# Moving the stores of converted weights from SyncE's DMA queue to GpSimd's

## The chip, the cores and the metric

One core of a Trainium2 chip runs the whole program. The metric is the device time of one execution in microseconds; lower is better. The engines named below are PE (TensorE), DVE (VectorE), ACT (ScalarE), POOL (GpSimd) and SP (SyncE, which here only issues DMAs).

## The reference

Attention over 4 batches and 8 heads of 576 positions with 64 columns, under a banded mask (32 positions wide in half of the heads; every fourth of 128 positions in the others), then two layers of matrix products on the 2304 tokens:

```
scores = scale * np.matmul(q, k.transpose(0, 1, 3, 2))      # masked, softmax
x = attn @ v                                                # -> (2304, 512)
x = (x @ w_a) * (x @ w_b) @ w_out                           # d_ff 1536
h = x @ w_in                                                # d_ff 2048
out = (max(h, 0) + alpha * min(h, 0)) @ w_out2
```

The weights of the two layers arrive as 64-bit floats. The kernel turns them into 32-bit floats on the chip, and each 32-bit number into a high and a low part, so that a product is three matmuls (high by high, high by low, low by high).

## The kernel before

The tokens are cut into tiles of 512, 512, 512 and 768. Attention of the first 512 tokens comes first; then the first layer runs over tile 0, 1 and 2 (12 blocks `f` of 128 columns of d_ff each), and the attention of the next tile is done in between, in 12 groups per tile. After that come the first layer for the last 768 tokens and the second layer for all of them, both by another scheme of products on halves.

While tile 0 is computed, the first layer's weights are converted, block by block: 24 pieces of `w_a` and `w_b` (two for each `f`, `job_w`) and 12 of `w_out` (`job_o`), 36 conversions in all. One conversion (`convert`) is: a load of 512 KB into one of four places of `raw_ring` (L194, issued by SP, kept in program order among the loads); two ACT passes over it (L176, L179) and two DVE passes (L183, L186) that leave 32-bit floats in one of five places of `cf_ring`; the split into high (ACT, L244) and low (DVE, L247) parts, in buffers from which PE reads; and then `then`, a store to DRAM. For `job_w` the 32-bit floats go to `wad` (L258, 256 KB, read from the place in `cf_ring`), for `job_o` the split pair goes to `wod` (L268, 512 KB, read from one of two places of `wo_ring`). Both are read back later: `wod` for tiles 1 to 3 (L277, L629), `wad` for the last tile (L597).

A place of `cf_ring` is written again by the L176 of the fifth conversion after it, a place of `wo_ring` by the L244 of the next but one `job_o`; both must wait until the store has read it.

SP's queue also carries the attention's inputs, in three places each: `in_qk` (L288) and `in_v` (L293). A load for the group three ahead can go only when PE has read that place, so SP stands at these for PE. An attention group is: scores (PE, L324), masking and maximum (DVE, L334, L340), exponentials (ACT, L345), normalisation (DVE, L352 to L354), transposition (PE, L361, into a tile named `tp`), copy (ACT, L366), product with v (PE, L374), placement (DVE, L399). From the second tile on, `visit` puts the transposition of one group, the values of the group before it and the scores of the next side by side on PE; this text calls that a visit, and names it by its `tp`.

The program is written as numbered steps, and a scheduler turns it into one fixed instruction order for each engine, from its own estimate of when inputs are ready. Each engine then runs its order strictly, waiting at semaphores. The tile names in the orders below: `pa`, `pb` and `accA` are PSUM banks, `sa` the bank that values and scores of a visit share, `ft` and `rt` the two large SBUF buffers.

Of the kernel before, what the change touches and what calls it, by code (L numbers as in the profile page):

```python
# [10 lines left out]
F32 = mybir.dt.float32  # L11
# [49 lines left out]
def tile_kernel(ctx: ExitStack, tc: tile.TileContext, qk, v, mask, wab, wo1, w2, alpha, out):  # L61
    nc = tc.nc
# [5 lines left out]
    wod = dram.tile([NFA, 128, 1024], F32, name="wod")  # L68
    wad = dram.tile([NFA, 128, 1024], F32, name="wad")
# [18 lines left out]
    def cut(t, first, *dims):  # L88
        size = int(np.prod(dims))
        ap = t[:, first:first + size]  # L90
        if len(dims) == 2:
            ap = ap.rearrange("p (a b) -> p a b", b=dims[1])
        elif len(dims) == 3:
            ap = ap.rearrange("p (a b c) -> p a b c", b=dims[1], c=dims[2])
        return ap
# [101 lines left out]
    def convert(src, dest, then=None, raws=raw_ring, places=cf_ring):  # L197
        raw = load_raw(src, raws)
        yield
        yield  # L200
        for f in float_of(raw, places):
            yield
        hi, lo = dest()
        split(hi, lo, f, nc.scalar, nc.vector)
        if then:
            then(f)
# [42 lines left out]
    ws, wo = {}, {}  # L249

    def job_w(k, f, j):
        def dest():
            if j == 0:
                ws[f] = cut(rt, 4096 + 2048 * f, 4, 512)
            return ws[f][:, 2 * j], ws[f][:, 2 * j + 1]

        def then(x):
            nc.sync.dma_start(out=wad[f, :, j * 512:(j + 1) * 512], in_=x)  # L258

        queue.append((k, convert(wab[f, j], dest, then)))  # L260

    def job_o(k, f):
        def dest():
            wo[0, f] = w = wo_ring.next().rearrange("p (h n) -> p h n", h=2)
            return w[:, 0], w[:, 1]

        def then(_):
            nc.sync.dma_start(out=wod[f], in_=wo[0, f].rearrange("p h n -> p (h n)").bitcast(F32))  # L268

        queue.append((k, convert(wo1[f], dest, then)))  # L270

# [636 lines left out]
```

## Time and profile before

| | us |
|---|---|
| median of 3 runs (lowest, highest) | 922.96 (922.65, 928.92) |
| the profiled execution, its time | 922.74 |
| the profiled execution, its span on the core | 920.8 |

The span is counted from the first to the last instruction of the core; the 1.94 us between span and time lie outside of it. Busy times of the profile are per engine; engines run side by side, so they don't add up. "Idle before ... <-" names what ended a wait.

### The profile page before, as it was taken

The numbers are of one execution on the slowest core, as the hardware profiler recorded it, in microseconds if no ns is written. First come the engines' busy times: TensorE is split into PE (matmuls) and PEld (weight loads), VectorE is DVE, ScalarE is ACT, GpSimd is POOL, SyncE is SP. The second block draws the span as 40 slices with busy tenths as digits, with TensorE's granted clock in tenths as the row PEclk, the third lists the DMA queues.
The fourth block names the chain that finished last, engine by engine and source line by source line (L and its number), as shares of the span: only waits on it lengthen the run. The fifth ranks groups of instructions, "written<-read, shape, count | busy, mean of one in ns | idle before, by whom it ended". The sixth has DMA issues, their size and how long they took to land.

```text
span 920.8 us, 15175 instructions
## 1 busy us (share of the span) xinstructions
PE 903.7 (98%) x5569; PEld 815.4 (89%) x5572; DVE 620.4 (67%) x1317; ACT 417.4 (45%) x967; POOL 0.7 (0%) x6
## 2 busy tenths in 40 slices
PE   8899999999999999999999999999999999999997
PEld 5677887887877888899999998999999999999997
DVE  5989986667666754669877589768565575555432
ACT  5887885555545543445445356233222242222221
POOL 0000000000000000000000000000000000000000
PEclk9999999999999999999999999999999999999999
DMA  7789895686777743553321988457434435344100
GB/s 212 250 286 331 303 335 200 197 278 222 237 257 263 234 163 109 204 199 132 129 93 67 331 287 297 140 158 231 126 115 142 121 115 161 115 145 129 59 35 34
DMA packets 76585, 171.24 MB, mean 186 GB/s; under 512 B 8672, under 2 KB 23776, under 8 KB 76512
## 3 DMA queue, kind: packets, MB, share of 16 engines
q1 hardware_dynamic: 76512, 170.28, 56.0%
q8 instruction: 44, 0.72, 0.3%
q14 instruction: 29, 0.24, 0.1%
HBM read 133.55 MB, written 36.70 MB: 185 GB/s over the span
## 4 chain that ended last, share of the span: by engine, by line
PE 85%; DMA 7%; DVE 4%; ACT 3%; issue 1%; SPq 0%; ACTq 0%; DVEq 0%
PE at L694 11%; PE pb L694 7%; PE pa L694 7%; PE accB L439 7%; PE accB L440 7%; PE accB L438 7%; PE accA L438 5%; PE accA L439 5%; PE accA L440 5%; DMA ft<-in_w 4%; PE pa L438 3%; PE pa L440 3%; PE pb L438 3%; PE pa L439 3%; PE pb L440 3%; PE pb L439 3%
## 5 line engine op out<-in xcount | busy, mean ns | idle before, releaser
L244 ACT CAST rt<-ft 128x512 fp32r<-128x512 f32 (+2 forms) x288 | 158.7, 560 | 271.0 <-PE accB L440 170.6
L247 DVE TENSOR_TENSOR rt<-ft,rt 128x512 fp32r<-128x512 f32 (+2 forms) x288 | 174.6, 613 | 121.1 <-ACT rt L244 109.0
L694 PE MATMUL at<-rt 128*128 128x384 f32 x648 | 130.9, 335 | 0.7 <-ACT ft L708 0.4
L438 PE MATMUL accB<-rt 128*128 128x384 f32 x384 | 127.6, 335 | 2.1 <-ACT ft L749 1.1
L439 PE MATMUL accB<-rt 128*128 128x384 f32 x384 | 128.4, 334 | 0.6 <-DVE rt L247 0.6
L440 PE MATMUL accB<-rt 128*128 128x384 f32 x384 | 128.0, 334 | 0.0
L694 PEld LDWEIGHTS at<-rt 128*128 128x128 f32 x648 | 113.8, 188 | 1.7 <-ACT ft L708 1.0
L708 ACT COPY ft<-at 128x384 f32<-128x384 f32 x108 | 51.6, 479 | 88.2 <-PE at L694 86.2
L438 PE MATMUL accA<-rt 128*128 128x512 f32 (+1 forms) x240 | 89.2, 373 | 0.5 <-ACT ft L749 0.5
L694 PE MATMUL pb<-rt 128*128 128x384 f32 x432 | 87.3, 336 | 1.2 <-DVE ft L705 1.2
L439 PE MATMUL accA<-rt 128*128 128x512 f32 (+1 forms) x240 | 88.4, 368 | 0.0
L440 PE MATMUL accA<-rt 128*128 128x512 f32 (+1 forms) x240 | 88.1, 368 | 0.0
L694 PE MATMUL pa<-rt 128*128 128x384 f32 x432 | 87.1, 334 | 0.0
L694 PEld LDWEIGHTS pb<-rt 128*128 128x128 f32 x432 | 75.5, 188 | 3.2 <-DVE ft L705 3.1
L694 PEld LDWEIGHTS pa<-rt 128*128 128x128 f32 x432 | 76.0, 188 | 0.0
L438 PEld LDWEIGHTS accB<-rt 128*128 128x128 f32 x384 | 71.9, 188 | 3.2 <-ACT ft L749 1.4
L439 PEld LDWEIGHTS accB<-rt 128*128 128x128 f32 x384 | 72.1, 188 | 1.0 <-DVE rt L247 1.0
L440 PEld LDWEIGHTS accB<-rt 128*128 128x128 f32 x384 | 72.0, 188 | 0.0
L183 DVE SCALAR_TENSOR_TENSOR ft<-ft 128x512 uint32<-128x512 uint32 x68 | 46.8, 689 | 28.5 <-ACT ft L179 27.9
L345 ACT ACTIVATE ft<-ft 128x96 f32<-128x96 f32 x144 | 52.4, 365 | 24.3 <-DVE ft L340 24.0
L705 DVE TENSOR_TENSOR ft<-ft,pb 128x384 f32<-128x384 f32 x72 | 39.7, 552 | 31.5 <-ACT ft L708 31.3
L176 ACT ACTIVATE ft<-ft 128x512 f32<-128x512 f32 x68 | 45.4, 668 | 29.0 <-DMA ft<-in_w 23.2
(80 smaller groups left out, 1377.0 us busy)
## 6 DMA issues: line engine op xcount, KB each, us to landing
rt<-wsd SPq DMA_DIRECT2D x168, 256.0 KB, 3.0
rt<-wod SPq DMA_DIRECT2D x48, 512.0 KB, 3.9
ft<-in_w SPq DMA_DIRECT2D x32, 512.0 KB, 5.0
wsd<-rt SPq DMA_DIRECT2D x56, 256.0 KB, 2.9
ft<-in_wab SPq DMA_DIRECT2D x24, 512.0 KB, 5.9
ft<-in_qk SPq DMA_DIRECT2D x48, 208.0 KB, 3.2
ft<-in_v SPq DMA_DIRECT2D x48, 144.0 KB, 3.2
wad<-ft SPq DMA_DIRECT2D x24, 256.0 KB, 5.0
```

The source lines that it names most:

```text
L176: nc.scalar.activation(f, high.bitcast(F32), AF.Abs, scale=2.0 ** -112)
L183: nc.vector.scalar_tensor_tensor(out=fi, in0=fi, scalar=3, in1=low, op0=ALU.logical_shift_left, op1=ALU.bitwise_or)
L244: hi_eng.copy(hi, x)
L247: lo_eng.tensor_tensor(out=lo, in0=x, in1=hi.bitcast(F32), op=ALU.subtract)
L345: nc.scalar.activation(self.et[:, s], self.st[:, s], AF.Exp, bias=self.sm[:, 0, s:s + 1], accum_out=self.sm[:, 1, s:s + 1])
L438: nc.tensor.matmul(acc, lhsT=wh, rhs=rh, start=first, stop=False)
L439: nc.tensor.matmul(acc, lhsT=wh, rhs=rl, start=False, stop=False)
L440: nc.tensor.matmul(acc, lhsT=wl, rhs=rh, start=False, stop=last)
L694: nc.tensor.matmul(acc[:, :HT], lhsT=a, rhs=x[:, b, c], start=start and c == k == 0, stop=c == 1 and k == 2, skip_group_check=not start,)
L705: nc.vector.tensor_tensor(out=out, in0=x, in1=acc[:, :HT], op=ALU.add)
L708: nc.scalar.copy(out, acc[:, :HT])
```

## The change

The two `then` functions issue their stores on POOL's queue (`nc.gpsimd`) instead of SP's (`nc.sync`). Sizes, places, sources and the place in the program text are the same.

```diff
 def job_w(k, f, j):
     ...
         def then(x):
-            nc.sync.dma_start(out=wad[f, :, j * 512:(j + 1) * 512], in_=x)
+            nc.gpsimd.dma_start(out=wad[f, :, j * 512:(j + 1) * 512], in_=x)
     ...
 def job_o(k, f):
     ...
         def then(_):
-            nc.sync.dma_start(out=wod[f], in_=wo[0, f].rearrange("p h n -> p (h n)").bitcast(F32))
+            nc.gpsimd.dma_start(out=wod[f], in_=wo[0, f].rearrange("p h n -> p (h n)").bitcast(F32))
```

The scheduler, which estimates anew, also gives other orders on the compute engines for a stretch of the program: on ACT, DVE and PE the orders are the same up to the last groups of the first attention and again from the end of tile 0 on, and differ in between.

On SP, the place of the third load of a conversion (the first `in_wab` row here) and of the fourth, before:

```order
L288 DMA ft<-in_qk 128x416 x2
L258 DMA wad<-ft 128x512
L293 DMA ft<-in_v 96x384
L194 DMA ft<-in_wab 128x512
L293 DMA ft<-in_v 96x384
L288 DMA ft<-in_qk 128x416
L258 DMA wad<-ft 128x512
L194 DMA ft<-in_wab 128x512
```

And the same place on SP in the changed kernel:

```order
L288 DMA ft<-in_qk 128x416
L194 DMA ft<-in_wab 128x512
L293 DMA ft<-in_v 96x384
L288 DMA ft<-in_qk 128x416
L293 DMA ft<-in_v 96x384
L288 DMA ft<-in_qk 128x416
L194 DMA ft<-in_wab 128x512
```

The stores are gone; the third load has moved ahead of an `in_qk` and an `in_v` load as well, while the fourth still follows the same `in_v` and `in_qk` loads.

On ACT, at the end of the first attention, one piece of the difference (L176 and L179 are the passes of the third conversion, L345 with the L366 of `tp_8` belong to attention groups):

```order
 L179 ACTIVATE ft<-ft 128x512
 L366 COPY ft<-tp_7_356 96x384
+L176 ACTIVATE ft<-ft 128x512
+L179 ACTIVATE ft<-ft 128x512
 L345 ACTIVATE ft<-ft 128x96 x3
 L366 COPY ft<-tp_8_395 96x384
 L244 CAST rt<-ft 128x512
-L176 ACTIVATE ft<-ft 128x512
-L179 ACTIVATE ft<-ft 128x512
```

The third conversion's two passes now stand ahead of three exponentials and the copy of `tp_8`, where before they stood behind them.

On PE, in tile 0, the visit that begins with `tp_3`, before:

```order
L439 MATMUL accA_3_662<-rt 128x512
L440 MATMUL accA_3_662<-rt 128x512
L438 MATMUL pa<-rt 128x512
L361 MATMUL tp_3_832<-ident,ft 96x128 x3
L374 MATMUL sa_836<-ft 64x64 x6
L324 MATMUL sa_836<-ft 64x96 x6
L439 MATMUL pa<-rt 128x512
```

And the same visit on PE in the changed kernel:

```order
L438 MATMUL pb<-rt 128x512
L439 MATMUL pb<-rt 128x512
L361 MATMUL tp_3_832<-ident,ft 96x128 x3
L374 MATMUL sa_836<-ft 64x64 x6
L324 MATMUL sa_836<-ft 64x96 x6
L440 MATMUL pb<-rt 128x512
L438 MATMUL accA_0_659<-rt 128x512
```

The visit has moved from behind the 12 products into `accA` and one into `pa` to ahead of them, 14 matmuls of 512 columns earlier. Counted so, the visits of tile 0 from `tp_0` to `tp_9` stand 4 later, then 4, 7, 14, 10, 5 and 9 earlier, the same, 8 earlier, and the same; the last two, `tp_10` and `tp_11`, haven't moved.

## Rows read from the trace of the kernel before

**Rows 1.** The page, part 1: busy us of each engine.

```profile
span 920.8 us, 15175 instructions
...
PE 903.7 (98%) x5569; PEld 815.4 (89%) x5572; DVE 620.4 (67%) x1317; ACT 417.4 (45%) x967; POOL 0.7 (0%) x6
```

**Rows 2.** Windows: stretch, its length, busy us (count) by engine, clock, DMA share, GB/s.

```profile
20.00:30.00 10.00, 8.57 (x106) 5.91 (x104) 9.51 (x33) 8.48 (x29) 0.00 (x0) 1.00 0.82 258
30.00:80.00 50.00, 47.49 (x333) 36.00 (x333) 44.09 (x108) 40.88 (x106) 0.00 (x0) 1.00 0.86 289
80.00:140.00 60.00, 60.00 (x394) 48.52 (x392) 54.68 (x121) 49.24 (x118) 0.00 (x0) 1.00 0.90 316
140.00:160.00 20.00, 20.00 (x116) 15.88 (x115) 13.66 (x29) 10.22 (x22) 0.00 (x0) 1.00 0.55 198
```

**Rows 3.** Waits of SP's queue, 0 to 160 us: total us, times, longest.

```profile
SPq L268 <- DVE rt L247: 29.5, 12, 4.7
...
SPq L258 <- DVE ft L353: 9.7, 7, 2.4
```

**Rows 4.** Timeline of SP around the third and fourth load: start, us, what.

```profile
23.80 1.32 SPq L288 DMA_DIRECT2D ft<-in_qk  x2
25.17 0.43 SPq L258 DMA_DIRECT2D wad<-ft  x1
25.70 0.37 SPq L293 DMA_DIRECT2D ft<-in_v  x1
26.11 0.46 SPq L194 DMA_DIRECT2D ft<-in_wab  x1
...
29.68 0.36 SPq L258 DMA_DIRECT2D wad<-ft  x1
30.09 0.42 SPq L194 DMA_DIRECT2D ft<-in_wab  x1
```

**Rows 5.** Timeline of ACT at the same place.

```profile
26.39 0.65 ACT L176 ACTIVATE ft<-ft 128x512 f32<-128x512 f32 x1
...
27.49 0.46 ACT L366 COPY ft<-tp 96x384 f32<-96x384 f32 x1
29.08 0.37 ACT L345 ACTIVATE ft<-ft 128x96 f32<-128x96 f32 x1 [1.13 <-DVE ft L340]
...
30.17 0.45 ACT L366 COPY ft<-tp 96x384 f32<-96x384 f32 x1
```

**Rows 6.** DMA issues (issuer, count, KB, median us to landing), then in_wab's minimum, median, maximum.

```profile
ft<-in_wab SPq DMA_DIRECT2D x24, 512.0 KB, 5.9
...
wad<-ft SPq DMA_DIRECT2D x24, 256.0 KB, 5.0
...
DMA to landing us min/median/max: 3.5/5.9/7.9
```

**Rows 7.** Timeline of PE at its waits; idle time before in brackets.

```profile
30.68 0.57 PE L374 MATMUL ap<-ft 96*64 96x64 f32 x12 [1.03 <-ACT ft L366]
...
34.12 0.50 PE L438 MATMUL pa<-rt 128*128 128x512 f32 x1 [0.31 <-ACT rt L453]
...
37.09 0.50 PE L438 MATMUL acc<-rt 128*128 128x512 f32 x1 [0.28 <-ACT rt L244]
...
77.54 0.39 PE L440 MATMUL pb<-rt 128*128 128x512 f32 x1
77.77 0.39 PE L438 MATMUL accA<-rt 128*128 128x512 f32 x1
79.03 0.50 PE L361 MATMUL tp<-ident,ft 128*96 128x128 f32 x3 [0.88 <-DVE ft L354]
```

**Rows 8.** Timeline of DVE: end of a group's chain; last read of a conversion.

```profile
78.43 0.46 DVE L354 TENSOR_TENSOR ft<-ft 128x288 f32<-128x288 f32 x1
...
126.58 0.69 DVE L186 SCALAR_TENSOR_TENSOR ft<-ft 128x512 uint32<-128x512 uint32 x1
```

**Rows 9.** Timeline of ACT: the fifth conversion after that one.

```profile
138.20 0.67 ACT L176 ACTIVATE ft<-ft 128x512 f32<-128x512 f32 x1
```

## The prediction

> **What bounds the kernel now.** I read the page's busy line first: PE is busy 903.7 of a span of 920.8 us, at a share of 98% [rows 1], so whatever a change gives back must be taken from the 17.1 us in which PE is idle, and whatever it costs must show as new idle time on PE. The windows then say where the stretch of the change stands [rows 2]: the first of the 36 stores goes at 25.17 [rows 4], and the conversions still run at 138 [rows 9]. From 80 us on PE has no idle time there at all, at the full granted clock; between 20 and 30 us it idles 1.43 us and between 30 and 80 us 2.51 us. DVE is the next engine: it has 5.91 us free of 50 and then 5.32 of 60. The DMA engines are 0.86 to 0.90 busy. SP's own waits come third: it stood 29.5 us at `wod` stores and at least 9.7 us at `wad` stores, waiting for DVE [rows 3], with loads queued behind it. Last I read PE's waits one by one: none names a DMA; they name ACT and DVE work that stands late in the conversions or in an attention group [rows 7].
>
> **What the change can give.** It removes 36 issues of 0.36 to 0.43 us [rows 4] from SP, and the waits in front of them. SP isn't on the path to the end, so this is worth only what an earlier load is worth. The loads don't run free: they still stand behind `in_qk` and `in_v` loads that wait for PE, and each needs one of four raw places that DVE's L186 must have left. The fourth load shows the size: behind its `in_v` and `in_qk` loads, SP is free at 29.68 instead of 30.09, 0.4 us earlier [rows 4]. The third gains more, because the new order also puts it ahead of an `in_v` and an `in_qk` load: the first of the two `in_qk` rows at 23.80 takes some 0.4 us as its neighbours do, so the load goes at about 24.2 instead of 26.11 [rows 4].
> The end of the gain is the idle time that PE has from its wait at 30.68 on: 2.51 us in 30 to 80 plus the 0.35 of that wait that lie before 30, against none at the other end. Two of these waits are for casts of weights, 0.31 and 0.28 us [rows 7]; I take these two as gone, **-0.6 us**, since half a microsecond of earlier loads is just enough for them, and leave the attention's waits to the terms below. From 80 to 160 us an earlier load buys nothing: PE is full there.
>
> **What the new ACT order costs.** ACT now meets the third conversion's L176 right after the copy at 27.49, that is at 27.95, and behind it stand the exponentials that before began at 29.08 and the copy at 30.17, whose end PE waited for at 30.68 [rows 5, 7]. An `in_wab` load lands 3.5 to 7.9 us after its issue, 5.9 in the median [rows 6]. Issued at 24.2 it is there at 27.7, 30.1 or 32.1. The two passes take 1.10 us (26.39 to 27.49, [rows 5]). So the exponentials begin at 29.08 as before, or at 31.2, or at 33.2: 0, 2.1 or 4.1 us later, and PE, which idles there already, waits that much longer. In return this conversion itself is earlier (its L176 was behind all that). Between 0 and 2.1 I take **+1.5 us**, nearer the median landing, because the queue ahead of this load is shorter than the median one's by a store; 0 and +4.1 stay as ends.
>
> **What the new PE order costs.** PE takes the visits of tile 0 earlier. A visit's transposition needs the group's L354 on DVE, and how close that is shows at 79.03, where PE waited 0.88 us for an L354 that ended at 78.89 [rows 7, 8]. A matmul of 512 columns takes 0.23 us (77.54 to 77.77, [rows 7]). What counts is the stretch between two visits, from one group's scores to its transposition: counted in the two orders, from `tp_0` to `tp_8` it shrinks by 8, 3 and 7 matmuls, grows by 4 and 5, shrinks by 4, grows by 9, shrinks by 8. On DVE the same groups have 10, 8, 6, 3, 5, 8, 4, 7 conversion and product passes between L334 and L354 before and 7, 6, 5, 6, 7, 6, 5, 4 after, so most of the shorter stretches have a shorter chain to fit, at 0.69 us of DVE for a pass [rows 8]. Twice it doesn't fit: `tp_3` loses 7 matmuls (1.6 us) for one pass (0.7), 0.9 us late; `tp_4` gains 4 (0.9) for three more passes (2.1), 1.2 late. Against that stands the 0.88 us wait at 79.03, which is the wait at `tp_4` and is in part the same time: 0.9 + 1.2 - 0.88 leaves 1.2, and I take **+0.9 us**, since DVE's passes overlap their neighbours a little. The ends are -0.9 (that wait goes and nothing comes) and, if the chains weren't shortened at all, the sum of what shrinks, 30 matmuls, +6.9.
>
> **What the stores cost on POOL.** POOL has 0.7 us of work in the whole program [rows 1], so nothing queues there but the stores themselves, in the order in which the conversions end. The trace shows no DMA issued by POOL. From below the nearest row is SP's issue, 0.36 us; from above the whole landing of a store, 5.0 us [rows 4, 6]. What covers either: a place of `cf_ring` is written again by the fifth conversion after it. The closest of these that I found among 31 is an L186 that ends at 127.27 with the next L176 in the place at 138.20 [rows 8, 9], 10.9 us, so a store may take 5.9 us more than the median 5.0 before ACT waits for it; `wo_ring`'s places have more. Waits added on ACT and DVE are for these places only. `wad` and `wod` are read back only after the last conversion. I cost this at **0**, with the ends under the rivals.
>
> **Sum.** 922.74 for the profiled execution, -0.6 +1.5 +0.9 = **924.5 us**; the median of the runs stands 0.2 us above the profiled one, which I neglect. That is no change: a measurement of this kernel can tell about 1% (9.2 us).
>
> **Rivals.**
> *Faster.* The third load lands before ACT needs it, the waits at casts and the 0.88 us go, and no visit is late. For it speaks that the orders were made for each other; against it, that PE has only 2.9 us to give. Time: 922.74 - 2.5 = 920.2, at best 919.9.
> *Visits wait.* DVE's chains keep their old length because DVE is at 88 to 91% and takes its rows late, and PE stalls at each shrunken stretch: +6.9 +1.5 = 931.1. It decides from the point where L354 ends later than the matmuls ahead of it, which at 79.03 it did already. Against it: the shorter DVE chains counted above.
> *Stores late.* If a store issued by POOL takes over 10.9 us from L186 to landing, ACT waits at L176, and PE runs dry behind it. At 15 us that is 4.1 us over for one round of five places, seven rounds, 29 us at most and some 14 if half is hidden: 937. The Trainium skill's page "SBUF — State Buffer" (the box on the DVE trap) speaks for it: descriptors of a POOL-issued DMA are written by the GpSimd cores, which certain DVE copies lock out, and it tells of a transfer of 620 ns taking 3100 ns. By that figure, as an estimate, a store would be 2.5 us later, within the 5.9 above; no trace here shows it.
> *DVE held.* POOL's preparation of a store blocks DVE, which has 11.2 us free between 30 and 140 us [rows 2]. It decides from 11.2 / 36 = 0.31 us a store. At an SP issue of 0.43 us it costs 36 x 0.43 - 11.2 = 4.3 (927); at 1.5, between that and the 5.0 of a landing, 43 (966). Nothing in this trace shows DVE sharing anything with POOL, which is idle. The same page of the Trainium skill (Who interferes with whom) says that a DVE instruction with two SBUF inputs contends with a GpSimd instruction that reads SBUF, not with one that only writes it. The conversions' DVE passes are of that two-input kind; so by that rule the chance is small, and no run here shows it yet.
> *Without effect.* The raw places, not the stores, hold the loads, and the orders come out even: 922.7, inside the forecast's own range.
>
> **How the numbers follow.** Forecast with its ends (922 to 928): 0.56, the case without effect included. Faster (919 to 922): 0.17. Visits wait (928 to 933.7 with the ACT term at its end): 0.15. Stores late 0.06, DVE held 0.06. Over 932.2 lie most of the last two and a little of the visits: 0.12. Under 913.7 nothing of the above reaches: 0.01. The rest, 0.87, is within 1%. The range 919 to 931 leaves out the last two cases and the upper part of the visits, some 0.16.
>
> **What would show it.** In the profile of the changed kernel: a second DMA queue with 12.6 MB; no L258 or L268 among SP's waits; ACT's idle before the third L176 naming `in_wab`, and PE's wait at the copy of `tp_8` near 32 us instead of 30.68; PE waits for L354 at `tp_3` and `tp_4`; PE without idle time from 90 to 160 us; DVE's pass L186 still at 0.69 us. I am wrong if ACT's L176 or L244 wait for stores, if DVE's passes are longer, or if PE's busy time itself changes.

## The result and the profile after

The changed kernel takes 935.52 us (median of 4 runs, 933.55 to 937.24); the kernel before, 923.11 in the same series. The ratio is 1.0112, with a 95% interval of 1.0085 to 1.0138: it is slower by about 1.1%, 11 us over the forecast and 4.5 us over the end of its range. The profiled execution took 933.55.

The page, part 1, as in [rows 1]:

```profile
span 931.8 us, 15181 instructions
...
PE 909.4 (98%) x5572; PEld 817.5 (88%) x5572; DVE 617.7 (66%) x1317; ACT 417.4 (45%) x967; POOL 20.2 (2%) x42
```

The span grew by 11.0 us. PE is idle 22.4 us of it for 17.1, and its busy time is 5.7 us longer with the same matmuls (three of them, some 0.6 us, are missing from the record of before), which no idle time explains. Windows show where both lie, as [rows 2] did (busy us and count of PE, PEld, DVE, ACT, POOL; then granted clock, DMA share, GB/s):

```profile
30.00:160.00 130.00, 119.23 (x777) 92.05 (x776) 104.21 (x246) 94.90 (x234) 18.87 (x35) 0.97 0.79 270
...
34.00:36.00 2.00, 1.44 (x20) 1.33 (x22) 1.82 (x6) 1.85 (x9) 0.00 (x0) 0.54 0.27 111
36.00:38.00 2.00, 2.00 (x13) 1.43 (x12) 1.65 (x9) 0.36 (x2) 0.00 (x0) 0.50 0.38 120
38.00:40.00 2.00, 2.00 (x6) 1.20 (x4) 0.00 (x0) 1.50 (x4) 0.00 (x0) 0.50 0.19 63
40.00:42.00 2.00, 2.00 (x18) 1.60 (x18) 1.91 (x6) 1.72 (x8) 0.00 (x0) 0.75 0.03 9
```

Between 30 and 160 us PE is idle 130 - 119.23 = 10.8 us, where before it was 2.5 [rows 2]: 8.3 us. From 34 to 42 it ran at half to three quarters of its clock: 1.44 x 0.46 + 2 x 0.50 + 2 x 0.50 + 2 x 0.25 = 3.2 us. Together 11.5 us, some of which later stretches gave back. Of the 5.7 us of longer busy time, 3.2 are the clock's here and some 0.6 the missing records; I haven't placed the rest. The DMA engines moved less per microsecond there than before, not more.

ACT's timeline at the third conversion, for [rows 5]:

```profile
27.04 0.67 ACT L176 ACTIVATE ft<-ft 128x512 f32<-128x512 f32 x1
...
28.14 0.48 ACT L366 COPY ft<-tp 96x384 f32<-96x384 f32 x1
31.88 0.66 ACT L176 ACTIVATE ft<-ft 128x512 f32<-128x512 f32 x1 [3.26 <-DMA ft<-in_wab]
...
34.05 0.46 ACT L366 COPY ft<-tp 96x384 f32<-96x384 f32 x1
```

SP's timeline ahead of it, for [rows 4]:

```profile
24.45 0.43 SPq L288 DMA_DIRECT2D ft<-in_qk  x1
24.92 1.51 SPq L194 DMA_DIRECT2D ft<-in_wab  x1
26.54 0.38 SPq L293 DMA_DIRECT2D ft<-in_v  x1
```

And PE's timeline behind it and at the visits, for [rows 7]:

```profile
34.56 0.91 PE L374 MATMUL ap<-ft 96*64 96x64 f32 x12 [4.26 <-ACT ft L366]
...
38.64 0.63 PE L438 MATMUL pb<-rt 128*128 128x512 f32 x1
39.06 0.63 PE L439 MATMUL pb<-rt 128*128 128x512 f32 x1
39.49 0.63 PE L440 MATMUL pb<-rt 128*128 128x512 f32 x1
...
53.61 0.53 PE L361 MATMUL tp<-ident,ft 128*96 128x128 f32 x3 [0.59 <-DVE ft L354]
...
71.66 0.50 PE L361 MATMUL tp<-ident,ft 128*96 128x128 f32 x3 [1.31 <-DVE ft L354]
...
96.95 0.50 PE L361 MATMUL tp<-ident,ft 128*96 128x128 f32 x3 [1.62 <-DVE ft L354]
```

The reader sees one chain: the third load goes at 24.92, nearly as forecast, takes 1.51 us to issue and is there some 6.9 us after its start; ACT stands 3.26 us at L176 with the exponentials and the copy of `tp_8` behind it; PE waits 4.26 us for that copy, 3.2 more than the 1.03 of before. The same twelve matmuls that took 0.57 us at 30.68 [rows 7] then show 0.91.

This wait isn't the only one of its kind. ACT's waits for the loads of conversions, 0 to 180 us (total, times, longest), and SP's waits in the same stretch:

```profile
ACT ft L176 <- DMA ft<-in_wab: 17.2, 13, 3.3
...
ACT ft L176 <- DMA ft<-in_wo: 5.9, 5, 1.8
```

```profile
SPq L293 <- PE sa L374: 60.5, 12, 7.8
SPq L194 <- DVE ft L186: 18.9, 12, 3.6
```

Eighteen conversions make ACT wait 23.1 us in all. Before, in the same stretch, the same two lines came to 2.8 us:

```profile
ACT ft L176 <- DMA ft<-in_wo: 2.5, 2, 2.1
...
ACT ft L176 <- DMA ft<-in_wab: 0.3, 1, 0.3
```

No store stands among SP's waits any more, where [rows 3] had 39 us of them. Between 30 and 160 us no wait listed for PE or DVE names a DMA; the late loads reach them through ACT.

The stores themselves, by the DMA issues (issuer, count, KB, median us to landing), for [rows 6]:

```profile
ft<-in_wab SPq DMA_DIRECT2D x24, 512.0 KB, 5.7
...
wad<-ft POOLq DMA_DIRECT2D x24, 256.0 KB, 5.4
...
wod<-rt POOLq DMA_DIRECT2D x12, 512.0 KB, 5.1
```

And one line of the view on L258, and one of that on L186, where the three times are minimum, median and maximum in ns:

```profile
L258 POOL DMA_DIRECT2D wad<-ft x24: 539/539/684, 25.3 to 146.4; - x24
```

```profile
L186 DVE SCALAR_TENSOR_TENSOR ft<-ft x68: 681/685/694, 24.3 to 589.5; 128x512 uint32<-128x512 uint32 x68
```

A store takes POOL 0.54 us and lands in 5.4 or 5.1 us; DVE's pass is as long as it was [rows 8]. Nobody waited for a store.

### The profile page after: what moved, and what is told of

Its sections match the earlier page's. It is cut to its first block, busy times and chain, and to the rows that moved or that the text cites. A ratio compares the mean times of both kernels' runs of the same rounds, so it can differ in the third digit from the quotient of the medians.

```text
span 931.8 us, 15181 instructions
## 1 busy us (share of the span) xinstructions
PE 909.4 (98%) x5572; PEld 817.5 (88%) x5572; DVE 617.7 (66%) x1317; ACT 417.4 (45%) x967; POOL 20.2 (2%) x42
## 4 chain that ended last, share of the span: by engine, by line
PE 83%; DMA 9%; DVE 4%; ACT 3%; issue 1%; SPq 0%; ACTq 0%; DVEq 0%
PE at L694 11%; PE pb L694 7%; PE pa L694 7%; PE accB L439 7%; PE accB L440 7%; PE accB L438 7%; PE accA L438 5%; PE accA L439 4%; PE accA L440 4%; DMA ft<-in_wab 3%; PE pb L438 3%; PE pa L438 3%; PE pb L439 3%; PE pb L440 3%; PE pa L440 3%; DMA ft<-in_w 3%
## 5 line engine op out<-in xcount | busy, mean ns | idle before, releaser
L176 ACT ACTIVATE ft<-ft 128x512 f32<-128x512 f32 x68 | 45.6, 671 | 50.3 <-DMA ft<-in_w 25.4
L345 ACT ACTIVATE ft<-ft 128x96 f32<-128x96 f32 x144 | 52.4, 367 | 23.5 <-DVE ft L340 23.2
```

The lines of the kernel that those rows point to most:

```text
L176: nc.scalar.activation(f, high.bitcast(F32), AF.Abs, scale=2.0 ** -112)
L345: nc.scalar.activation(self.et[:, s], self.st[:, s], AF.Exp, bias=self.sm[:, 0, s:s + 1], accum_out=self.sm[:, 1, s:s + 1])
```

## The experiments

Two theories stood at the start. **A**: the changed orders cost the time; the queue of the stores costs nothing. **B**: stores prepared and issued by POOL cost it. Every run is compared with the kernel before on the same chip, whose median lay between 924.1 and 925.9 us; the ratio carries the reading. Old orders are those of the kernel before, new ones those of the changed kernel.

| run | stores on | orders | us, median | ratio to before, 95% |
|---|---|---|---|---|
| d1_dup | SP, and again on POOL | old | 937.68 | 1.0123 (1.0067 to 1.0179) |
| d2_late1 | POOL, the first on SP | near the new | 931.36 | 1.0086 (1.0054 to 1.0117) |
| d3_early3 | SP, the first three on POOL | new at first | 928.77 | 1.0046 (1.0024 to 1.0069) |
| d4_wod | SP, `wod` on POOL | old at first | 932.12 | 1.0077 (1.0050 to 1.0103) |
| e1_pool_old | POOL | old | 922.47 | 0.9963 (0.9942 to 0.9985) |
| e2_sp_new | SP | new | 938.63 | 1.0124 (1.0084 to 1.0163) |
| e3_pool_new | POOL | new | 937.44 | 1.0116 (1.0067 to 1.0164) |
| e4_dup16 | SP, and 16 columns on POOL | old | 926.43 | 1.0009 (0.9985 to 1.0034) |
| f1_act_back | POOL | new, but a piece of ACT's | 935.03 | 1.0094 (1.0075 to 1.0113) |
| f2_act_forward | POOL | old, but that piece and SP's | 932.60 | 1.0069 (1.0048 to 1.0090) |
| f3_pe_old | POOL | new, PE's old | 947.08 | 1.0219 (1.0173 to 1.0266) |
| f4_sp_order | POOL | old, SP's new | 927.02 | 1.0026 (1.0001 to 1.0051) |
| g1_load_new | POOL, loads too | new | 940.67 | 1.0174 (1.0126 to 1.0222) |
| g2_load_old | POOL, loads too | old | 929.35 | 1.0062 (1.0038 to 1.0087) |
| h1_ready_new | POOL, data ready | new | 925.11 | 0.9984 (0.9960 to 1.0009) |
| h2_ready_old | POOL, data ready | old | 923.45 | 0.9990 (0.9969 to 1.0011) |

**The stores twice.** Likewise for `wod`; the orders of PE, ACT, DVE and SP stay those of before.

```diff
         def then(x):
             nc.sync.dma_start(out=wad[f, :, j * 512:(j + 1) * 512], in_=x)
+            nc.gpsimd.dma_start(out=wad2[f, :, j * 512:(j + 1) * 512], in_=x)
```

> The kernel before, in which POOL issues a second copy of each of the 36 stores into spare DRAM, 12.6 MB more; the orders of PE, ACT and DVE are those of before, and SP still issues its own 36 stores. The output is the same. Theory A (the changed orders cost the time, the stores on POOL's queue as such nothing): within 3 us of the kernel before, 922 to 926, the upper part for 12.6 MB more traffic; no PE wait of over 1.1 us between 26 and 40 us. Theory B (preparation of the stores by POOL, or their queue, costs the time): at least the 12.4 us of the change, 933 or more, with longer DVE passes or ACT waits for places.

It came out on B's side, 937.68. But the windows and the issues of this run point to a third cause, which neither theory had:

```profile
30.00:160.00 130.00, 120.86 (x791) 92.93 (x792) 106.45 (x246) 96.01 (x235) 18.53 (x35) 1.00 0.97 360
```

```profile
ft<-in_wab SPq DMA_DIRECT2D x24, 512.0 KB, 7.3
```

The DMA engines are 0.97 busy (0.79 in the changed kernel), a load lands in 7.3 us for 5.9 [rows 6], and ACT waits for `in_wab` 15 times, 13.1 us in all. So this run can't tell B from traffic (**C**); e4 had to.

**One store back, three stores moved, only `wod` moved.** Each is one line, in this order:

```diff
-            nc.gpsimd.dma_start(out=wad[f, :, j * 512:(j + 1) * 512], in_=x)
+            (nc.sync if 2 * f + j < 1 else nc.gpsimd).dma_start(out=wad[f, :, j * 512:(j + 1) * 512], in_=x)
```

> The changed kernel with only the first store of w_a's first piece back on SP, 35 stores on POOL. The third load stands in its old place on SP, and ACT's order is that of before up to the third conversion and beyond. Theory A, with the early loss of about 7.5 us put down to the third conversion's place: PE waits about 1 us instead of 4.26 at the copy of tp_8, the granted clock stays at 1.00 from 30 to 45 us, and the time falls by some 7 us to 926 to 930; what the later visits lose (about 5 us) may stay. Theory B: 35 of 36 stores are still POOL's, so 935 as changed.

```diff
-            nc.sync.dma_start(out=wad[f, :, j * 512:(j + 1) * 512], in_=x)
+            (nc.gpsimd if 2 * f + j < 3 else nc.sync).dma_start(out=wad[f, :, j * 512:(j + 1) * 512], in_=x)
```

> The kernel before with only the first three stores (of w_a and w_b) issued by POOL, 33 stores on SP. Its orders are those of the changed kernel through the third conversion. Theory A: the early loss comes back nearly whole with 3 of 36 stores, PE idle of about 4 us before the values at tp_8's copy and a granted clock near 0.5 behind it; 929 to 933. Theory B: a twelfth of the cost, 924.

```diff
-            nc.sync.dma_start(out=wod[f], in_=wo[0, f].rearrange("p h n -> p (h n)").bitcast(F32))
+            nc.gpsimd.dma_start(out=wod[f], in_=wo[0, f].rearrange("p h n -> p (h n)").bitcast(F32))
```

> The kernel before with the 12 stores to wod (512 KB each, half of the bytes) issued by POOL and the 24 to wad by SP. Orders are those of before until well after the third conversion. Theory A: no early loss; what the later visits lose depends on the orders that come out, 922 to 929. Theory B: half of the bytes, or a third of the stores, on POOL give a third to a half of the cost, 927 to 929, spread over the whole of tile 0, with no change in which engine waits at tp_8's copy.

A single store of 36 back on SP took 2 to 3 us off by the ratios (their intervals overlap), and three of 36 alone put 4 us on, so the cost doesn't go by the number of stores. PE's timeline of d3 shows the early loss that A had written down, 3.3 us of idle time for its 4, and its windows the clock behind it:

```profile
32.97 0.91 PE L374 MATMUL ap<-ft 96*64 96x64 f32 x12 [3.32 <-ACT ft L366]
```

```profile
34.00:36.00 2.00, 2.00 (x15) 1.45 (x14) 2.00 (x9) 0.77 (x5) 0.00 (x0) 0.50 0.37 111
```

But d2 came out 1.4 us above A's range and d4 3 us above it, though neither has the early order: a loss at one place isn't all. Every one of these kernels also had orders of its own, so that the queue and the order weren't yet apart.

**Order and queue apart.** The two kernels hold the same instructions, of which 36 differ in their queue. So the order of one can be written into the other: a table lists the instructions by number for each engine, over the stretch in which the two orders differ, and an edge of issue order, without a wait, ties each to the one before. For SP it is the whole row of its DMAs but the 36 stores, in place of the rule that keeps the loads in program order.

```diff
-        tc.keep_in_program_order(nc.sync.dma_start(out=raw.bitcast(I64), in_=src))
+        nc.sync.dma_start(out=raw.bitcast(I64), in_=src)
...
+def pin(tc):
+    traced = {i.name: i for i in tc.nc.cur_bb.bb.instructions}
...
+                if last:
+                    tc.add_manual_dep(traced[name], last, how, reason="order")
+                last = name
```

> The changed kernel, all 36 stores on POOL, with the orders of PE, ACT, DVE and of SP's loads written out as they are in the kernel before. Theory A (the changed orders cost the time): as the kernel before or a little faster, 920 to 925, with PE's wait at the copy of tp_8 near 1 us. Theory B (stores on POOL's queue cost it, whatever the order): as the changed kernel, 933 to 937, which the doubled stores (937.7 with the old orders) speak for.

> The kernel before, all 36 stores on SP, with the orders of PE, ACT, DVE and of SP's loads written out as they are in the changed kernel. Theory A: as the changed kernel, 933 to 938, the upper part since the stores on SP now hold loads that this order wants early. Theory B: as the kernel before, 922 to 926.

> The changed kernel itself once more, beside the two with written orders on the same chip: 933 to 938 by either theory; its distance from the kernel with the old orders is the cost of the orders, its distance from the one with the stores on SP the cost of the queue.

This decides between A and B. With the old orders 36 stores on POOL cost nothing (922.47, even 0.4% under before); with the new orders the time is 938.63 with the stores on SP and 937.44 with them on POOL. On POOL the orders make 937.44 - 922.47 = 15.0 us; the queue takes off 3.5 us under the old orders, and the 1.2 us under the new are within the noise (1.0116 and 1.0124, with intervals that nearly coincide). In e1, over the same stretch as above:

```profile
30.00:160.00 130.00, 127.93 (x841) 100.64 (x840) 112.91 (x259) 100.97 (x248) 18.86 (x35) 1.00 0.84 288
```

PE is idle 2.1 us for 2.5 before, at the full clock. e1 is also the version that beats both kernels; its fastest run (922.17) is no faster than the fastest of before in that series (922.14), but its slowest of 11 is 925.02 where before reached 933.94. Why it varies less was not tried.

**Small stores.** The doubled store again, with 16 columns of 512:

```diff
+            nc.gpsimd.dma_start(out=wad2[f, :, j * 512:j * 512 + 16], in_=x[:, :16])
```

> The kernel before, its 36 stores on SP and its orders unchanged, with 36 more stores issued by POOL that write only 16 of the columns, 128 pieces of 64 bytes into spare DRAM. The output is the same. This is the doubled store without its 12.6 MB. If preparation by POOL cost the doubled stores their 12 us (theory B), it costs it here: 933 or more. If it was the traffic, with loads landing in 7.3 us for 5.9 (theory C), the time is that of before, 922 to 926.

926.43 beside 925.92: no difference (1.0009). The same number of stores from POOL without the bytes costs nothing, and POOL is as busy with them between 30 and 160 us, 18.53 us in both runs; so the 12 us of d1 are traffic. That it reaches the time through late loads is read from ACT's waits in d1, and not tried.

**Which part of the orders.** In f1 one piece of ACT's new order is undone; f2 is its mirror, the old orders with this piece in the new place (and SP's loads in the new order):

```diff
 L366 COPY ft<-tp_7_356 96x384
-L176 ACTIVATE ft<-ft 128x512
-L179 ACTIVATE ft<-ft 128x512
 L345 ACTIVATE ft<-ft 128x96 x3
 L366 COPY ft<-tp_8_395 96x384
 L244 CAST rt<-ft 128x512
+L176 ACTIVATE ft<-ft 128x512
+L179 ACTIVATE ft<-ft 128x512
```

> The changed kernel with all its orders written out, but for one piece of ACT's: the two passes of the third conversion (L176, L179) stand again behind the three exponentials, the copy of tp_8 and one cast, as in the kernel before. Theory A1 (that place alone makes the early loss of about 7.5 us, idle time and low clock together): 928 to 930, PE's wait at the copy of tp_8 near 1 us and the clock at 1.00 from 30 to 45 us. Theory A2 (loads are late all along under the new orders, and the third conversion only shows it first): the loss is made up behind it, 933 to 936.

> The mirror of the last one: stores on POOL, PE, DVE and the rest of ACT in the old orders, SP's loads in the new one, and on ACT the third conversion's two passes ahead of the exponentials and the copy of tp_8. Theory A1: the 7.5 us come onto the 922.5 of the old orders, 929 to 931, with PE idle 3 to 4.5 us at the copy of tp_8. Theory A2: the old orders leave the loads so much time that the wait is caught up, 923 to 926.

f1 went as A2 had it, 935.03. Its PE timeline:

```profile
30.59 0.57 PE L374 MATMUL ap<-ft 96*64 96x64 f32 x12 [1.03 <-ACT ft L366]
37.09 0.79 PE L438 MATMUL pa<-rt 128*128 128x512 f32 x1 [2.83 <-ACT rt L453]
```

The wait at `tp_8` is 1.03 as before, and the next conversion's load makes one of 2.83 us at the next place. f2 came out at 932.60, over both of its ranges and 10 us over e1, where A1 had 7 to 8. Its PE timeline shows two waits:

```profile
34.62 0.91 PE L374 MATMUL ap<-ft 96*64 96x64 f32 x12 [4.26 <-ACT ft L366]
...
51.30 0.75 PE L438 MATMUL pa<-rt 128*128 128x512 f32 x1 [3.12 <-ACT rt L453]
```

The first is the piece's. The second isn't: f4, below, has SP's new order without the piece, and the same wait stands there, 2.30 us. So f2 is the sum of two causes, and the piece alone costs 932.60 - 927.02 = 5.6 us over f4 by the medians, 4 by the ratios. It is enough for a loss by itself, but by f1 taking it away doesn't help where later conversions press as well. A1, my theory of one early place as the whole cause of the early loss, fell with f1.

Then PE's old order among the new ones, and SP's new order among the old ones:

> Stores on POOL, the new orders on ACT, DVE and for SP's loads, but PE's old order, in which the visits of tile 0 stand later. If the visits moved earlier cost the other 5 us (theory A1), the time is 929 to 932 with the early loss in it and PE's waits for L354 between 60 and 100 us at under 1 us in all, for 4.1 in the changed kernel. By theory A2 PE waits for casts (L244, L247) instead and the time stays at 934 to 938.

> Stores on POOL, the old orders on PE, ACT and DVE, and the new order of the loads on SP, in which the third load goes two places earlier and 16 loads change places. Under A1 and A2 alike the order of the loads alone costs nothing while ACT reaches them late: 921 to 924. A time over 930 would say that the order of the loads on SP, and not the orders of the compute engines, makes the loss.

Both edits are tables of the kind above. f3 took 947.08, the slowest of all and 9 us over the upper of its two ranges: PE's new order, with its earlier visits, fits the other new orders, and the old one doesn't; PE waits 4.0 us for L354 in f3 too. f4 is 4.5 us over e1 by the medians, 3 beyond the range written for it, and its PE timeline names one wait more:

```profile
45.36 0.79 PE L438 MATMUL pa<-rt 128*128 128x512 f32 x1 [2.30 <-ACT rt L453]
```

ACT had waited 2.42 us for an `in_wab` load at 43.60: SP's new row issues the seventh load of a conversion ahead of the fifth, which ACT needs first under the old orders. So the order of the loads alone has a part, smaller than that of all the orders together (15.0 us).

**Loads on POOL.**

```diff
-        raw = places.next()
-
-        tc.keep_in_program_order(nc.sync.dma_start(out=raw.bitcast(I64), in_=src))
+        raws, raw = places, places.next()
+
+        (nc.gpsimd if raws is raw_ring else nc.sync).dma_start(out=raw.bitcast(I64), in_=src)
```

> The changed kernel, its orders on PE, ACT and DVE written out, with the 36 loads of conversions issued by POOL too, so that they no longer stand behind the in_v and in_qk loads that wait for PE on SP; SP keeps the rest in the same order. Theory H1 (the loads are held behind these waits): ACT's waits for in_wab and in_wo before 180 us fall from 23 to under 8 us and the time comes down to 924 to 929. Theory H2 (the four places are free too late for these orders): the loads wait for DVE's L186 instead, ACT waits as long, and the time stays at 933 to 938.

> The same with the old orders on PE, ACT and DVE: stores and conversion loads on POOL. H1 and H2 alike: 920 to 923, since PE has only some 2 us of idle time left between 30 and 160 us under these orders; a time over 926 would say that loads on POOL's queue cost something by themselves, behind stores that wait for DVE.

Inconclusive on H1 and H2. ACT's waits for loads fell from 23 to 11.8 us, but both kernels gained a new loss at their start, where PE now waits for the first attention inputs; that POOL's loads hold these up is likely and not shown. PE's timeline of g2:

```profile
12.47 0.71 PE L324 MATMUL sp<-ft 64*64 64x96 f32 x12 [2.71 <-DMA ft<-in_qk]
```

Such waits in the first 30 us make most of the 7 us by which g2 lies over e1: PE is busy 23.09 us of them, 27.72 in e1. And on POOL the loads now stand behind stores that wait for DVE, as they did on SP before the change. Whether a load could be earlier under the new orders stays open. g1 is still 11.3 us over g2, so the orders cost what they cost.

**No wait for data.** The loads are taken out of the conversions' way, not out of the program: the second load fills two of the four raw places, the third another, and 33 write as many bytes into spare DRAM (`n` counts the loads; a load goes to `to` instead of `raw`).

```diff
+        to = {1: raw, 2: ft[:, 5120:7168], 3: ft[:, 7168:8192]}.get(n, wad[NFA + n - 4] if n > 3 else None)
...
```

> The changed kernel, orders written out, in which no conversion from the third on waits for its load: the first three loads fill all four raw places, and the later 33 write their 512 KB into spare DRAM instead. So the weights computed from the third conversion on aren't the reference's; number, size and place of DMAs and all work of the engines stay. Theory L (late loads are the whole cause): no ACT wait for in_wab, PE idle between 30 and 160 us at most 3 us, clock at 1.00 there, 920 to 925. Theory O (the orders also lose time against each other): 928 or more, with PE waiting for L354 and L244 although ACT waits for no load.

> The same under the old orders of PE, ACT and DVE, with the same part of the computation changed: 919 to 923 by either theory, the floor against which the run with the new orders is read.

This closes it, on L's side. Under the new orders and with the stores on POOL, over the same stretch:

```profile
30.00:160.00 130.00, 127.87 (x838) 99.92 (x837) 110.82 (x259) 100.13 (x245) 18.87 (x35) 1.00 0.82 288
```

and PE's timeline:

```profile
31.18 0.57 PE L374 MATMUL ap<-ft 96*64 96x64 f32 x12 [1.03 <-ACT ft L366]
35.09 0.50 PE L438 MATMUL pa<-rt 128*128 128x512 f32 x1 [0.27 <-ACT rt L453]
```

Idle time of PE is 2.1 us instead of 10.8, none of it for L354, the clock is 1.00, and the time is 925.11 beside 923.45 with the old orders, 1.7 us that are within the noise (0.9984 and 0.9990). h1 also frees SP of its waits for L186, so that the attention's loads behind them go earlier; but in the changed kernel PE and DVE waited for no such load. The new orders are as good as the old while the data is there; with loads as they really land, they are 15 us worse.

## Why the prediction was wrong

**The failed step** is "What the new ACT order costs". Its mechanism was right: ACT meets L176 before the load has landed, and the exponentials and copies behind it keep PE waiting. The term was mis-sized: +1.5 us, with +4.1 as its end, where the runs show about 12 to 15 for the orders; the one piece that it priced, the third conversion, measured 4 to 5.6 by f2 over f4. Three things made it so.

- At the place itself the load went at 24.92, 0.7 later than estimated, and landed after 6.9 us, beyond the median of 5.9, while I had counted on a little less than the median [rows 6]; 3.2 us of idle time, not 1.5. That alone lies within the ends.
- I priced one conversion. Of the others the prediction only said that "From 80 to 160 us an earlier load buys nothing"; that a load may come too late for a new order had no term there. But the orders differ through most of tile 0, and 18 conversions waited. In the old order the loads were there (ACT waited under 3 us in all). f1 shows that the loss goes on from place to place when the first is mended; h1, that late loads are all of it.
- The clock had no term. 4.26 us of idle PE were followed by 8 us at 0.50 to 0.75, 3.2 us of loss. PE's busy time changed by it, which the prediction had named as a sign of being wrong.

**The new PE order**, +0.9: the waits for L354 came, 4.1 us of them for the 0.9 of [rows 7], but not by the step's mechanism. h1 has the same order on PE and DVE and waits for no L354, so the shortened stretches fit their chains, and also the wait of before at `tp_4` is gone there. In the changed kernel DVE is late since ACT is late. The term by itself is nothing that stands clear of the noise (h1 beside h2); that f3, with the visits put back, is slower still says the same.

**SP's gain**, -0.6: e1 has it nearly pure. PE's idle time falls by 0.4 us and the waits for casts, which the term counted as gone, are still there, 0.2 to 0.4 us each. What is gone is the 0.88 us wait at `tp_4`, which stood in the PE order's term. The size was about right by luck, not by the mechanism.

**POOL's stores**, 0: right, by e1 and e4. Landing rose from 5.0 to 5.4 and from 3.8 to 5.1 us, inside the 5.9 us of slack, and nothing waited; the longest landing of a store from POOL was 7.4 us, 8.4 in e1, for the 10.9 that it had.

**The rivals.** Visits wait (931.1, or 933.7) came near in its number, by late loads and not by DVE's chains. Stores late and DVE held are refuted by e1: no wait for a store, DVE's passes at 0.68 us. The prediction's sentence on the two-input passes, from the Trainium skill's page "SBUF — State Buffer" (Who interferes with whom), agrees with that; the fivefold transfer that the page tells of (A bandwidth-pool intuition that's wrong) shows in no landing here, 8.4 us at the longest. The Trainium skill's page "DMA: Bandwidth & Descriptors" (Issuing engines are not separate DMA queues) says that issuing from several engines saves only the time of the issue, usually small; e1's fastest run beside that of before, 922.17 and 922.14, agrees.

That the scheduler's own estimate of SP's queue gave the old orders their slack, and that it went with the stores, is my reading of the code. The runs show the orders and what they cost, not why the scheduler chose them.

## What to carry to other kernels

A change of a DMA's queue is, under a scheduler that estimates, a change of the order of every engine; before its price is worked out from the queue, the engine that takes data first (ACT here) is gone through load by load, for how long before each use the load lands in the old order and in the new. Absence of waits in the trace before says only that the old order had slack, not how much. Where an edit is worth having for itself, the old order can be written out and kept: 922.5 instead of 937.4 us for the same queues.

## What was unexpected of the hardware

A wait of PE can cost more than its length. The granted clock went from 1.00 to 0.50 behind idle times of 4.26 us (changed kernel, and f2), 3.32 (d3), 3.12 (f2), 2.83 (f1), 2.30 (f4), and even behind 1.85 (d2). But it stayed at 1.00 behind the 1.31 and 1.62 us in the changed kernel, 2.25 in d4, and 2.47 and 2.64 in f3; the length of one wait doesn't decide it in these runs. At 0.50 the products at 38.64, 39.06 and 39.49 of the changed kernel's timeline follow each other every 0.42 us, for the 0.23 of [rows 7]: the two levels, 1.2 and 2.4 GHz. The Trainium skill's page "TensorE: Matmul & The Clock Gate" (Wait — 56ns, not 53.3ns?) gives 426.7 and 215.7 ns from start to start for 512 columns, which agrees with the first and lies a little under the second.

Issuing a load took SP 0.33 to 0.46 us as a rule, but 1.51 for the third load; f1 issued the same load in 0.47, and the kernel before took 1.49 for one at 106.89. Nothing in the profile says why, and nothing here was tried on it.
